# Two 64-token chunks a stage, in 64-row tiles, from stage 8 on

## The chip, the cores and the metric

The kernel runs on one core of a Trainium2 chip. The metric is the device time of one execution in microseconds. A core has five engines that run side by side: TensorE (PE, with its weight loads shown as PEld), VectorE (DVE), ScalarE (ACT), GpSimd (POOL) and SyncE (SP); DMA queues move data between the chip's memory and the core's.

## The reference

```python
# r, k, v: (batch 4, heads 8, tokens 768, 48), w, u: (8, 48), all fp32
state = np.zeros((B, H, D, D))
for t in range(S):
    cur = np.einsum('bhd,bhe->bhde', u[None] * kt, vt)
    y[:, :, t] = np.einsum('bhd,bhde->bhe', rt, state + cur)
    state = w[None, :, :, None] * state + np.einsum('bhd,bhe->bhde', kt, vt)
x = y.transpose(0, 2, 1, 3).reshape(B * S, H * D)      # 3072 tokens, 384 wide
h = x @ w_in                                           # 384 -> 2048
out = np.maximum(0.01 * h, h) @ w_out                  # 2048 -> 384
```

A linear attention with a decaying state per head (`w` the decay, `u` the weight of the token itself), then a two-layer network with a leaky rectifier over all 3072 tokens.

## The kernel before

The tokens are cut into 24 stages of 128 tokens (`L`): stage n is tokens 128 (n div 4) of batch n mod 4. So stage n + 4 takes over the state that stage n leaves. Each stage does, by its letters in the order below:

- `k`, `r`, `v` (line 241): loads, issued by GpSimd, each into a place of its own (24 places).
- `P` (390): VectorE scales r and k by powers of the decay. `X..T` (395): SyncE issues a DMA that turns both into `tp` (head dimension on the partitions); in the first stages TensorE turns them (`T`).
- `q` (419, 421, 423): VectorE forms each token's weight for itself, summed over the head dimension (`s_tok`); `Q` (430): GpSimd spreads it on the diagonal of the score tile `at`.
- `A` (482): TensorE multiplies k by r: 128x128 scores for each of 8 heads, in 8 matmuls, two of which use different halves of the rows. `M` (495): VectorE copies the part above the diagonal into `at`, two heads' halves a stage.
- `K` (523): TensorE forms the product of keys and values, 4 matmuls of 96 columns, two heads each. `S` (589, 591): VectorE adds the old state and multiplies by the decay of 128 tokens (`wl`).
- `Y` (621): TensorE forms the output, turned: 12 matmuls with the old state (`st`) as stationary operand and 16 with the values (`v_sb`), each 32 columns of the array wide and 128 columns long. `y` (635): ScalarE copies it into `xT`.
- `G`, `J` (660) and `g`, `j` (671): first layer. A `J` block is two stages (256 tokens) by two of 16 feature blocks, 6 matmuls of 256 columns; eight of them make a pair of stages. ScalarE does the rectifier.
- `H` (684) and `h` (696): second layer, one stage, 16 matmuls of 384 columns; ScalarE copies the result out, SyncE stores it.

From stage 8 on the stages go in pairs. A pair is: scores of both stages, `H`, outputs of both, key-value products of both, `H`, eight `J` blocks; from pair 7 on the scores come after the third `J`. Pairs are numbered by half their first stage: pair 4 is stages 8 and 9, pair 11 is stages 22 and 23. Stages 20 to 23 need no key-value product, since nothing follows them.

The program is written out in one list, `ORDER`; every engine runs its own instructions in the order of that list, and a small planner (`Sched`) puts in the semaphore waits: what reads waits for its writer, what writes for writer and readers. TensorE's results go to 8 banks, handed out at build time in the order of the list: `take` pops the front of a queue, `give` appends to its end. A bank is reused when its last reader is done.

```python
free = list(range(8))
def take():
    i = free.pop(0)
    return ps[i], ("ps", i)
def give(key):
    free.append(key[1])
```

Of the kernel before, what the change touches and what calls it, by code (L numbers as in the profile page):

```python
# [6 lines left out]
ALU = mybir.AluOpType  # L7
# [6 lines left out]
L = 128  # L14
# [11 lines left out]
TURNED, DIAG, CARRY, EXACT, RAW = 6, 4, 4, 1, 1  # L26
# [3 lines left out]
Q0 Y0 t3k P0k r3 P3q M1a T3q r2 P2q y0 k2 K0 M1b v1 Q1 W G0.1 Y1 t3q X3 wi3 A3 y1 g0.1 S3 T2q D3 G1.1 g1.1 k5 t2q r5 r4  # L30
P2k T2k wi2 S0 v2 M3b t2k Q3 G0.3 g0.3 G1.3 k4 M3a Y3 P5k A2 y3 P4q T4q v4 wi0 T5k v5 wo3 t4q g1.3 G3.1 q5 t5k Q5 G3.3
g3.3 P5q r6 wo2 X2 g3.1 M2b D2 wo1 G3.2 Q2 G0.2 g0.2 T5q t5q K2 P4k T4k M2a t4k S2 G1.2 g3.2 q4 Q4 K1 S1 Y2 A5 A4 G1.0
y2 G2.1 M5a G0.0 G2.3 M4a M5b Y5 g0.0 y5 M4b Y4 y4 G2.2 g2.2 K4 J2.4 j2.4 k6 wo0 J2.1 J2.2 g1.0 g1.2 S4 k7 P6q q6 j2.1
P6k P7k G2.0 r7 q7 X6T J2.6 j2.6 J2.3 j2.3 k8 G3.0 J2.7 j2.7 k9 r9 j2.2 J2.5 P7q g3.0 g2.3 X7T J2.0 H1 h1 r8 q8 g2.0 Q6
P9k j2.0 P8k H0 j2.5 H3 Q7 A6 P9q X9T P8q X8T v6 A7 M6a v7 M7a g2.1 H2 h2 v9 v11 v10 M6b Y6 M7b y6 Q8 q9 Y7 y7 K5 r11
K6 S6 r10 k10 S5 Q9 v8 K7 S7 h0 h3 k11 J3.0 j3.0 J3.1 j3.1 J3.2 j3.2 J3.3 j3.3 J3.4 j3.4 J3.5 j3.5 J3.6 j3.6 J3.7 j3.7
A8 A9 M8a M8b M9a M9b P10q P10k X10T P11q P11k X11T k12 r12 v12 k13 r13 v13 q10 Q10 q11 Q11 H4 h4 Y8 Y9 y8 y9 K8 K9 S8
S9 H5 h5 J4.0 j4.0 J4.1 j4.1 J4.2 j4.2 J4.3 j4.3 J4.4 j4.4 J4.5 j4.5 J4.6 j4.6 J4.7 j4.7 A10 A11 M10a M10b M11a M11b
P12q P12k X12T P13q P13k X13T k14 r14 v14 k15 r15 v15 q12 Q12 q13 Q13 H6 h6 Y10 Y11 y10 y11 K10 K11 S10 S11 H7 h7 J5.0
j5.0 J5.1 j5.1 J5.2 j5.2 J5.3 j5.3 J5.4 j5.4 J5.5 j5.5 J5.6 j5.6 J5.7 j5.7 A12 A13 M12a M12b M13a M13b P14q P14k X14T  # L40
P15q P15k X15T k16 r16 v16 k17 r17 v17 q14 Q14 q15 Q15 H8 h8 Y12 Y13 y12 y13 K12 K13 S12 S13 H9 h9 J6.0 j6.0 J6.1 j6.1
J6.2 j6.2 P16q P16k X16T P17q P17k X17T A14 A15 J6.3 j6.3 M14a M14b M15a M15b k18 r18 v18 k19 r19 v19 J6.4 j6.4 J6.5
j6.5 J6.6 j6.6 J6.7 j6.7 q16 Q16 q17 Q17 H10 h10 Y14 Y15 y14 y15 K14 K15 S14 S15 H11 h11 J7.0 j7.0 J7.1 j7.1 J7.2 j7.2
P18q P18k X18T P19q P19k X19T A16 A17 J7.3 j7.3 M16a M16b M17a M17b k20 r20 v20 k21 r21 v21 J7.4 j7.4 J7.5 j7.5 J7.6
j7.6 J7.7 j7.7 q18 Q18 q19 Q19 H12 h12 Y16 Y17 y16 y17 K16 K17 S16 S17 H13 h13 J8.0 j8.0 J8.1 j8.1 J8.2 j8.2 P20q P20k
X20T P21q P21k X21T A18 A19 J8.3 j8.3 M18a M18b M19a M19b k22 r22 v22 k23 r23 v23 J8.4 j8.4 J8.5 j8.5 J8.6 j8.6 J8.7
j8.7 q20 Q20 q21 Q21 H14 h14 Y18 Y19 y18 y19 K18 K19 S18 S19 H15 h15 J9.0 j9.0 J9.1 j9.1 J9.2 j9.2 P22q P22k X22T P23q
P23k X23T A20 A21 J9.3 j9.3 M20a M20b M21a M21b J9.4 j9.4 J9.5 j9.5 J9.6 j9.6 J9.7 j9.7 q22 Q22 q23 Q23 H16 h16 Y20 Y21
y20 y21 H17 h17 J10.0 j10.0 J10.1 j10.1 J10.2 j10.2 A22 A23 J10.3 j10.3 M22a M22b M23a M23b J10.4 j10.4 J10.5 j10.5
J10.6 j10.6 J10.7 j10.7 H18 h18 Y22 Y23 y22 y23 H19 h19 J11.0 j11.0 J11.1 j11.1 J11.2 j11.2 J11.3 j11.3 J11.4 j11.4  # L50
J11.5 j11.5 J11.6 j11.6 J11.7 j11.7 H20 h20 H21 h21 H22 h22
# [92 lines left out]
def bass_rwkv5_eagle__then__act_leaky_relu_kernel(  # L144
# [19 lines left out]
    r_sb = SB("r_sb", [128, NST, HD])  # L164
    k_sb = SB("k_sb", [128, NST, HD])
    v_sb = SB("v_sb", [128, NST, H * E])
# [34 lines left out]
    sum_t = [SB(f"sum_t{i}", [128, NP, 2 * D]) for i in range(4)]  # L201
    xT = [SB(f"xT{i}", [128, NSL, 512]) for i in range(NX)]
# [31 lines left out]
    def load_one(n, which, pace=()):  # L234
        b, t0 = at_of(n)
        src = {"k": k, "r": r, "v": v}[which][b].rearrange("h t d -> t h d")[t0:t0 + L, :, :]
        if which == "v":
            dst = v_sb[:, n, :].rearrange("p (h e) -> p h e", e=E)[:, :, 0:D]
        else:
            dst = {"k": k_sb, "r": r_sb}[which][:, n, :].rearrange("p (h d) -> p h d", d=D)  # L240
        add("pool", lambda: G.dma_start(dst, src), R=pace, W=[(which, n)], dma=f"{which}{n}")  # L241
# [66 lines left out]

    def zero_v(n0, n1):
        add("dve", lambda: V.memset(v_sb[:, n0:n1, :].rearrange("p n (h e) -> p (n h) e", e=E)[:, :, D:E], 0.0),  # L310
            W=[("v0", n) for n in range(n0, n1)])
# [36 lines left out]
    def table(dst, exps, name, read):  # L348
        add("act", lambda: A.activation(dst[:, :], lnw[:, :], AF.Exp, scale=exps[:, 0:1]),
            R=["lnw", read], W=[name + "tab"])  # L350
# [30 lines left out]
    def k_of(n):  # L381
        return k_sb[:, n, :] if n >= EXACT else k_f[:, n, :]

    def r_of(n):
        return r_sb[:, n, :] if n >= EXACT else r_f[:, n, :]

    def prep_half(n, half):
        iq = n % NQK
        src, tab, name, done = ((r_of(n), qtab, "r", "qp"), (k_of(n), ktab, "k", "kp"))[half]
        add("dve", lambda: V.tensor_tensor(qk[iq][:, H * half:H * half + H, 0:D], hd(src), hd(tab[:, :]), ALU.mult),  # L390
            R=[(name, n), "qk"[half] + "tab", ("qk0", iq)], W=[(done, iq)])
# [16 lines left out]
    def scaled_v(n):  # L408
        iv = n % NVS
        ps_s, key = y_bank[n]  # L410
        s_of = ps_s[:, HD:HD + H]
        add("dve", lambda: V.tensor_tensor(hd(vs[iv][:, :]),
                                           v_sb[:, n, :].rearrange("p (h e) -> p h e", e=E)[:, :, 0:D],
                                           s_of.unsqueeze(2).to_broadcast([128, H, D]), ALU.mult),
            R=[("v", n), key], W=[("vs", iv)])
# [10 lines left out]
    def diag_tile(n):  # L426
        ia = n % NAT
        for hh in range(2):
            s_of = s_tok[n % 4][:, :].rearrange("p (m two) -> p two m", two=2)[:, hh, :]
            add("pool", lambda hh=hh, s_of=s_of: G.tensor_tensor(  # L430
                at[ia][:, hh, :, :], ident[:, :].unsqueeze(1).to_broadcast([128, NP, 128]),
                s_of.unsqueeze(2).to_broadcast([128, NP, 128]), ALU.mult),
                R=["ident", ("s", n % 4)], W=[("at", ia, hh)])

# [81 lines left out]
    def kv_mm(n):  # L516
        iq = n % NQK
        ps_kv, key = kv_bank[n] = take()
        carried = NB <= n < CARRY

        def emit():
            for p in range(NP):
                last = PE.matmul(ps_kv[:, 96 * p:96 * p + 96],  # L523
                                 qk[iq][:, H + 2 * p:H + 2 * p + 2, :].rearrange("p h e -> p (h e)"),
                                 v_sb[:, n, :].rearrange("p (h e) -> p h e", e=E)[:, 2 * p:2 * p + 2, 0:D],
                                 start=p == 0 or not carried, stop=not carried)
            if carried:
                last = PE.matmul(ps_kv[:, 0:HD], ident[:, :], st[n % NT][:, :, :].rearrange("p m e -> p (m e)"),
                                 start=False, stop=True)
            return last  # L530

        reads = [("kp", iq), ("v", n), ("qk0", iq)]
        if carried:
            reads += [("st", n % NT), "ident"]
        add("pe", emit, R=reads, W=[key])
# [37 lines left out]
    def decay_table():  # L573
        for hh in range(2):
            rows = slice(64 * hh, 64 * hh + D)
            add("act", lambda rows=rows, hh=hh: A.activation(
                wl[rows, :, hh * D:hh * D + D], wcol[rows, :].unsqueeze(2).to_broadcast([D, NP, D]), AF.Exp,
                scale=float(L)), R=["wcol", "wl"], W=[f"wl{hh}"])

    def state(n):  # L580
# [4 lines left out]
        if n < NB or n < CARRY:  # L585
            add("dve", lambda: V.tensor_tensor(new[:, :, :], kv, wl[:, :, :], ALU.mult),
                R=[key, "wl0", "wl1"], W=[("st", (n + NB) % NT)])
        else:
            add("dve", lambda: V.tensor_tensor(sum_t[n % 4][:, :, :], kv, st[n % NT][:, :, :], ALU.add),  # L589
                R=[key, ("st", n % NT)], W=[("sum", n % 4)])  # L590
            add("dve", lambda: V.tensor_tensor(new[:, :, :], sum_t[n % 4][:, :, :], wl[:, :, :], ALU.mult),  # L591
                R=[("sum", n % 4), "wl0", "wl1"], W=[("st", (n + NB) % NT)])

    def y_mm(n, ps_y, key):
        it, ia, iv, is_ = n % NTP, n % NAT, n % NVS, n % NT

        def strip(s, q):
# [5 lines left out]
            if kk < 2:  # L603
                one.append((v_sb[:, n, c0 + 32 * kk:c0 + 32 * kk + 32], at[ia][:, 0, p, :]))
            if kk > 0:
                c1 = c0 + 16 + 32 * kk
                one.append((v_sb[:, n, c1:c1 + 32], at[ia][:, 1, p, :]))
# [17 lines left out]
        reads = [("v", n), ("v0", n), ("at", ia, 0), ("at", ia, 1), "ident", ("tp", it, 0)]  # L625
# [64 lines left out]
    def g2_out(n, c0=0, c1=HD):  # L690
# [20 lines left out]
        "v0y": lambda: zero_v(NB, NST), "zr": zero_raw, "qk0": zero_qk, "wlz": zero_w,  # L711
# [3 lines left out]
        "Wl": log_columns, "C": decay_columns, "W": decay_table,  # L715
# [15 lines left out]
        "L": lambda n, x: load_stage(n),  # L731
# [73 lines left out]
```

## Time and profile before

| | us |
|---|---|
| median of 3 runs | 169.3 (169.16 to 169.36) |
| span of the profiled execution, first to last instruction | 166.8 |

The page gives the span and no other time for the profiled execution; the median is 2.5 us above it.

| engine | busy us | share of the span | instructions |
|---|---|---|---|
| TensorE, matmuls | 160.2 | 96% | 2076 |
| TensorE, weight loads | 120.6 | 72% | 2076 |
| VectorE | 107.6 | 64% | 224 |
| ScalarE | 89.0 | 53% | 168 |
| GpSimd | 111.0 | 67% | 125 |

How to read the lines that follow: a group line gives line and engine, operation, output and inputs, the shapes and the count, then busy us and the mean ns of one, then the engine's idle time in front of them and what ended it. The lines of the chain and of the timeline begin with the start in us and the length in us; several equal instructions in a row are one line (x16). Matmuls are pipelined: the length of one (some 0.2 us) is not what it costs, the distance between starts is. The granted clock of TensorE is full in all forty slices of the page but for rounding.

### The profile page before, as it was taken

What the parts mean: (1) busy time and instruction counts of PE and PEld (TensorE: products, weight loads), DVE (VectorE), ACT (ScalarE), POOL (GpSimd) and SP (SyncE); (2) the same over time, 40 slices, a digit from 0 to 9 for tenths busy, and PEclk for the clock granted to TensorE, in tenths of its full rate; (3) what the DMA queues carried; (4) which work ended last, traced back from release to release, by engine and by line L of the source; (5) the groups of instructions that cost most, each with busy time, mean ns of one, the idle gap of its engine ahead of it and who ended that gap; (6) DMA issues with size and microseconds to landing.
All of it is one profiled execution on the core that took longest, in us unless ns stands there. A gap on an engine that the chain in (4) does not pass through costs nothing.

```text
span 166.8 us, 4840 instructions
## 1 busy us (share of the span) xinstructions
PE 160.2 (96%) x2076; PEld 120.6 (72%) x2076; DVE 107.6 (64%) x224; ACT 89.0 (53%) x168; POOL 111.0 (67%) x125
## 2 busy tenths in 40 slices
PE   2899989999999999999999999999999999999994
PEld 2578879986567678678678678678678678678663
DVE  7799998478687695695699998865765705000000
ACT  3846973875048339339337437437437447449121
POOL 8999898978999949859759979896630630000000
PEclk9999999999999999999999999999999999999999
DMA  7999999999999994996994999999917011011012
GB/s 109 156 140 157 169 193 192 171 149 173 93 168 220 113 157 130 105 108 155 105 146 118 152 127 127 156 140 140 154 51 165 12 47 51 0 47 51 35 59 96
DMA packets 101267, 20.18 MB, mean 121 GB/s; under 512 B 94459, under 2 KB 101246, under 8 KB 101246
## 3 DMA queue, kind: packets, MB, share of 16 engines
q0 software_dynamic: 76512, 10.03, 95.0%
q1 hardware_dynamic: 23694, 9.65, 29.1%
q8 instruction: 16, 0.26, 0.7%
q10 hardware_dynamic: 1040, 0.20, 0.6%
q14 instruction: 5, 0.04, 0.1%
HBM read 20.45 MB, written 4.72 MB: 151 GB/s over the span
## 4 chain that ended last, share of the span: by engine, by line
PE 86%; POOL 7%; DMA 3%; DVE 2%; issue 0%; ACT 0%; POOLq 0%
PE ps L684 38%; PE ps L660 36%; PE ps L621 6%; DMA r_sb<-in_r_dram 3%; PE ps L482 3%; PE ps L523 2%; POOL r_sb L241 2%; POOL k_sb L241 2%; POOL v_sb L241 2%; POOL w_in_sb L251 1%; DVE prod L405 1%; DVE s_tok L423 0%; PE ps L453 0%; POOL trow L273 0%; DVE rku L421 0%
## 5 line engine op out<-in xcount | busy, mean ns | idle before, releaser
L660 PE MATMUL ps<-xT,w_in_sb 128*128 128x256 bf16 (+1 forms) x672 | 67.2, 257 | 0.0
L684 PE MATMUL ps<-w_out_sb,gT 128*128 128x384 bf16 (+2 forms) x400 | 65.6, 320 | 0.0
L671 ACT ACTIVATE gT<-ps 128x512 bf16<-128x512 f32 x96 | 56.3, 598 | 13.8 <-PE ps L660 9.7
L660 PEld LDWEIGHTS ps<-xT,w_in_sb 128*128 128x128 bf16 x672 | 57.1, 98 | 7.5 <-DVE sum_t L589 0.5
L430 POOL TENSOR_TENSOR at<-ident,s_tok 128x512 bf16<-128x512 bf16 x40 | 42.7, 1096 | 23.4 <-DVE s_tok L423 23.4
L684 PEld LDWEIGHTS ps<-w_out_sb,gT 128*128 128x128 bf16 x400 | 37.7, 98 | 22.4
L696 ACT ACTIVATE out_sb<-ps 128x384 f32<-128x384 f32 (+2 forms) x25 | 11.8, 477 | 54.5 <-PE ps L684 54.5
L495 DVE CAST_PREDICATED at<-mask,ps 128x512 bf16<-128x512 uint16 x40 | 24.9, 684 | 21.3 <-PE ps L482 21.2
L241 POOL DMA_DIRECT2D v_sb<-in_v_dram x24 | 22.1, 927 | 0.0
L241 POOL DMA_DIRECT2D k_sb<-in_k_dram x23 | 21.2, 925 | 0.0
L241 POOL DMA_DIRECT2D r_sb<-in_r_dram x23 | 21.1, 924 | 0.1
L421 DVE TENSOR_TENSOR rku<-r_sb,ku 128x384 bf16<-128x384 bf16 x20 | 13.8, 688 | 1.1 <-DMA r_sb<-in_r_dram 0.5
L589 DVE TENSOR_TENSOR sum_t<-ps,st 128x384 bf16<-128x384 f32 x16 | 8.8, 550 | 5.6 <-PE ps L523 5.6
L635 ACT ACTIVATE xT<-ps 128x384 bf16<-128x384 f32 x24 | 10.8, 490 | 2.6 <-PE ps L621 2.6
L423 DVE TENSOR_REDUCE s_tok<-rku 128x8 f32<-128x384 bf16 x20 | 11.1, 553 | 0.7
L591 DVE TENSOR_TENSOR st<-sum_t,wl 128x384 bf16<-128x384 bf16 x16 | 10.6, 664 | 0.6
L621 PE MATMUL ps<-at,v_sb 128*32 128x128 bf16 x384 | 10.8, 223 | 0.0
L390 DVE TENSOR_TENSOR qk<-k_sb,ktab 128x384 bf16<-128x384 bf16 x23 | 10.1, 444 | 1.1 <-DMA k_sb<-in_k_dram 1.1
L621 PEld LDWEIGHTS ps<-tp,st 128*32 128x32 bf16 x240 | 7.3, 96 | 3.0 <-issue 1.6
L621 PEld LDWEIGHTS ps<-at,v_sb 128*32 128x32 bf16 x384 | 8.8, 98 | 0.5 <-issue 0.2
L621 PE MATMUL ps<-tp,st 128*32 128x128 bf16 x240 | 9.1, 221 | 0.0
L390 DVE TENSOR_TENSOR qk<-r_sb,qtab 128x384 bf16<-128x384 bf16 x23 | 8.8, 386 | 0.2 <-DMA r_sb<-in_r_dram 0.2
(63 smaller groups left out, 92.9 us busy)
## 6 DMA issues: line engine op xcount, KB each, us to landing
out_dram<-out_sb SPq DMA_DIRECT2D x23, 192.0 KB, 2.2
v_sb<-in_v_dram POOLq DMA_DIRECT2D x24, 96.0 KB, 4.8
r_sb<-in_r_dram POOLq DMA_DIRECT2D x23, 96.0 KB, 4.7
k_sb<-in_k_dram POOLq DMA_DIRECT2D x23, 96.0 KB, 4.9
w_in_sb<-in_moe_w_in_dram POOLq DMA_DIRECT2D x4, 384.0 KB, 6.1
w_out_sb<-in_moe_w_out_dram POOLq DMA_DIRECT2D x4, 384.0 KB, 7.1
tp<-qk SPq DMA_TRANSPOSE x18, 5.3
k_f<-in_k_dram ACTq DMA_DIRECT2D x1, 192.0 KB, 2.8
```

The source lines that it names most:

```text
L241: add("pool", lambda: G.dma_start(dst, src), R=pace, W=[(which, n)], dma=f"{which}{n}")
L390: add("dve", lambda: V.tensor_tensor(qk[iq][:, H * half:H * half + H, 0:D], hd(src), hd(tab[:, :]), ALU.mult), R=[(name, n), "qk"[half] + ...
L421: add("dve", lambda: V.tensor_tensor(rku[i2][:, :], r_of(n), ku[i2][:, :], ALU.mult), R=[("r", n), ("ku", i2)], W=[("rku", i2)])
L423: add("dve", lambda: V.tensor_reduce(s_tok[i2][:, :], hd(rku[i2][:, :]), AX.X, ALU.add), R=[("rku", i2)], W=[("s", i2)])
L430: add("pool", lambda hh=hh, s_of=s_of: G.tensor_tensor(at[ia][:, hh, :, :], ident[:, :].unsqueeze(1).to_broadcast([128, NP, 128]), s_of.un ...
L495: add("dve", lambda: V.copy_predicated(at[n % NAT][:, hh, :, :], mask[:, :].bitcast(mybir.dt.uint16).unsqueeze(1).to_broadcast([128, NP, 1 ...
L621: last = PE.matmul(ps_y[32 * q:32 * q + 32, 128 * s:128 * s + 128], a, m, start=not whole and step == 0, stop=step == len(columns[q]) - 1)
L635: add("act", lambda: A.activation(xT[ix][:, :, 128 * slot:128 * slot + 128], ps_y[:, 0:HD].rearrange("p (s t) -> p s t", t=128), AF.Copy), ...
L660: last = PE.matmul(ps_g[:, step * f:step * f + step], w_in_sb[:, s, 128 * fb:128 * fb + 128], xT[ix][:, s, t], start=s == 0, stop=s == NSL ...
L671: add("act", lambda: A.activation(gT[ig][:, fb0:fb0 + count, t], ps_g[:, :].rearrange("p (f t) -> p f t", t=128 * width), AF.Prelu, alpha= ...
L684: last = PE.matmul(ps_o[:, 0:c1 - c0], gT[ig][:, s, 128 * slot:128 * slot + 128], w_out_sb[:, s, c0:c1], start=s == 0, stop=s == NFB - 1)
L696: add("act", lambda: A.activation(out_sb[io][:, c0:c1], ps_o[:, 0:c1 - c0], AF.Copy), R=[key], W=held)
```

## The change

From stage 8 on a stage is worked as two chunks of 64 tokens, with a state between them; two stages are handled together.

- Scores (`AA`): only the two 64x64 blocks on the diagonal are formed, 32 matmuls of 64x64 tiles by 64 columns a pair in place of 16 of 128 by 128. One mask operation (`MM`) covers both stages, so two a pair in place of four; the diagonal tiles on GpSimd have half the elements.
- Key-value products (`KK`): one for each chunk, 32 matmuls of 64x64 tiles by 48 columns a pair in place of 8 of 96; only the products of a head with itself. For stages 20 to 23 that of the first chunk is formed, where there was none. They come right after the scores, ahead of the outputs.
- State (`SM` after the first chunk, `SO` after the second): sum, product with the decay of 64 tokens in fp32, half as wide, and two copies that spread it to the old form for the outputs. Four a pair in place of two, of four operations (five for the first of stages 8 to 11) in place of two.
- Outputs (`YY`): 48 matmuls a pair with the states as stationary operand (128 rows, 32 columns wide, 64 long) in place of 24 of 128, then 64 with the values (64 rows, 32 wide, 64 long) in place of 32 of 128. The two chunks go to different banks.
- Order: the scores come after the fourth `J` block in all pairs; the preparation `P` and the transposes for the next pairs stand ahead of the scores from pair 5 on.
- Loads of k, r and v go into rings of 16 places, so stage n waits for the readers of stage n - 16.
- Before stage 8: tables of powers for 64-token chunks (`qtab2`, `ktab2`, `wlc`, `wl2`), a smaller mask and identity, and six memsets.

TensorE's matmuls go from 2076 to 2828. The order of one period before (pair 6) and after (pair 5):

```diff
-A12 A13 M12a M12b M13a M13b P14q P14k X14T P15q P15k X15T k16 r16 v16 k17 r17 v17 q14 Q14 q15 Q15 H8 h8
-Y12 Y13 y12 y13 K12 K13 S12 S13 H9 h9 J6.0 j6.0 J6.1 j6.1 ...
+J4.0 j4.0 J4.1 j4.1 J4.2 j4.2 P12q P12k X12T P13q P13k X13T J4.3 j4.3 AA5 KK5 J4.4 j4.4 MM5a MM5b SM10 SM11
+k14 r14 v14 k15 r15 v15 J4.5 j4.5 J4.6 j4.6 J4.7 j4.7 q12 Q12 q13 Q13 SO10 SO11 H6 h6 YY5 yy5a yy5b H7 h7
```

```diff
-            dst = v_sb[:, n, :].rearrange("p (h e) -> p h e", e=E)[:, :, 0:D]
+            dst = v_sb[:, n % NR, :].rearrange("p (h e) -> p h e", e=E)[:, :, 0:D]
...
-        add("pool", lambda: G.dma_start(dst, src), R=pace, W=[(which, n)], dma=f"{which}{n}")
+        add("pool", lambda: G.dma_start(dst, src), R=pace, W=[(which, n), (which, n - NR)], dma=f"{which}{n}")
...
+    def a_pair(j):
+        at_bank["pair", j] = (take(), take())
+        def emit():
+            for i in range(2):
+                it = (2 * j + i) % NTP
+                for p in range(NP):
+                    for hh in range(2):
+                        rows = slice(64 * hh, 64 * hh + D)
+                        for c in range(2):
+                            t = slice(64 * c, 64 * c + 64)
+                            x = 64 * (NP * i + p)
+                            last = PE.matmul(at_bank["pair", j][hh][0][t, x:x + 64], tp[it][rows, NP + p, t],
+                                             tp[it][rows, p, t], start=True, stop=True)
+            return last
...
+    def kv_pair(j):
+        chunks = range(2 if 2 * j + NB < NST else 1)
+        kv_bank["pair", j] = [take() for _ in chunks]
...
+                        for hh in range(2):
+                            t, x = slice(64 * c, 64 * c + 64), D * (NP * i + p)
+                            h = 2 * p + hh
+                            last = PE.matmul(kv_bank["pair", j][c][0][64 * hh:64 * hh + 64, x:x + D],
+                                             qk[n % NQK][t, H + h, :], v_sb[t, n % NR, E * h:E * h + D],
+                                             start=True, stop=True)
...
+    def half_state(n, c):
...
+            add("dve", lambda: V.tensor_tensor(both[:, :, :], kv, old[:, :, :], ALU.add), ...
...
+        add("dve", lambda: V.tensor_tensor(new[:, :, :], both[:, :, :], wlc[:, :, :], ALU.mult), ...
+        blocks(wide, new, name, at_)          # two copies of 64 partitions
+        if i == 1:
+            give(key)
...
+    def y_pair(j):
+        y_bank["pair", j] = (take(), take())
...
+                        for q in range(4):
+                            p, kk = divmod(4 * s + q, 3)
+                            mm(c, i, s, q, old[:, p, 32 * kk:32 * kk + 32], tp[n % NTP][:, p, 64 * c:64 * c + 64], False)
...
+                for step in range(4):
+                    for c in range(2):
+                        t = slice(64 * c, 64 * c + 64)
+                        for q in range(4):
+                            s, hh, c0, p = lists[q][step]
+                            last = mm(c, i, s, q, v_sb[t, n % NR, c0:c0 + 32], tile[t, hh, NP * i + p, :],
+                                      i == 1 and step == 3)
```

More of the change, by code (lines that the diff above doesn't have):

```diff
@@ L163, in bass_rwkv5_eagle__then__act_leaky_relu_kernel @@
     w_out_sb = SB("w_out_sb", [128, NFB, HD])
[L164 to L166 removed]
+    r_sb = SB("r_sb", [128, NR, HD])
+    k_sb = SB("k_sb", [128, NR, HD])
+    v_sb = SB("v_sb", [128, NR, H * E])
     w_row = SB("w_row", [128, HD // 2], FP32)
@@ new lines, in a_pair @@
+    def a_pair(j):
[12 more added lines that the diff above has]
+            return last
+        add("pe", emit, R=[("tp", (2 * j + i) % NTP, half) for i in range(2) for half in range(2)],
+            W=[key for _, key in at_bank["pair", j]])
```

234 lines of the change are left out of this document (179 added, 55 removed).

## The prediction

> **What bounds the kernel now.** I read the page first, then the chain of waits in order of time, then busy time by window, then the timeline of TensorE down to single groups of matmuls.
>
> ```profile
> span 166.8 us, 4840 instructions
> ...
> PE 160.2 (96%) x2076; PEld 120.6 (72%) x2076; DVE 107.6 (64%) x224; ACT 89.0 (53%) x168; POOL 111.0 (67%) x125
> ```
>
> The page says that TensorE is busy 96% of the span. A busy share can hide waits, so I look at one period of the part that the change touches. The chain in order of time, start and length in us:
>
> ```profile
> 95.78 0.89 PE ps L621 x56
> 96.67 0.45 PE ps L523 x8
> 97.12 2.60 PE ps L684 x16
> 99.72 1.97 PE ps L660 x18
> 101.68 0.55 PE ps L482 x16
> 102.24 3.38 PE ps L660 x30
> ...
> 108.22 0.90 PE ps L621 x56
> ```
>
> From one L621 (attention output) to the next it is all TensorE: 12.44 us for two stages, no other engine in the chain. Each piece fits a price per column. L684 streams 384 columns in 2.60/16 = 162.5 ns, L660 256 columns in 1.97/18 = 109.4 ns: 0.415 ns a column and some 3 ns fixed. So a 64-column matmul would stream in 29.6 ns. The four-up groups come from the timeline (start, length, count):
>
> ```profile
> 83.56 0.22 PE L621 MATMUL ps<-tp,st 128*32 128x128 bf16 x1
> 83.61 0.23 PE L621 MATMUL ps<-at,v_sb 128*32 128x128 bf16 x4
> 83.67 0.23 PE L621 MATMUL ps<-tp,st 128*32 128x128 bf16 x4
> ...
> 84.16 0.51 PE L523 MATMUL ps<-v_sb,qk 128*128 128x96 bf16 x8
> 84.51 2.76 PE L684 MATMUL ps<-w_out_sb,gT 128*128 128x384 bf16 x16
> ```
>
> Four matmuls into four 32-column strips last 0.23 us together where one lasts 0.22: they run side by side, one group each 56 ns (83.61 to 83.67). The 56 matmuls of L621 are 14 groups, 0.78 us; their piece is 0.89, so some 0.10 us is lost where the shape of the tiles changes. The 16 of L482 are 8 pairs at 56 ns, 0.45 us, and the piece is 0.55: the same 0.10. L523 takes (84.51 - 84.16)/8 = 43 ns each, 0.345 us. The check: L660 48 x 109.4 = 5.25, L684 32 x 162.5 = 5.20, scores 0.45, outputs 0.78, key-value 0.345, four changes of shape 0.40, sum 12.43 against 12.44. The stretch has no idle time to win back; only matmul time counts, and a wait that is added counts in full.
>
> **The change part by part.** The terms of the sum are made against the span of 166.8 us; the page gives this execution no time of its own beside it. The median of the runs is 169.3, so 2.5 us lie outside the span and I keep them.
>
> *Matmuls.* In groups that run at once, for a pair of stages. Scores: from 8 groups of two tiles by 128 columns to 8 groups of four 64x64 tiles by 64 columns. Key-value: from 8 single matmuls by 96 to 8 groups of four 64x64 tiles by 48. Outputs, state part: from 6 groups of four by 128 to 12 groups of four by 64. Outputs, value part: from 8 groups of four by 128 to 8 groups of eight 64x32 tiles by 64. Changes of shape: from four to five, the new one inside the outputs (128 rows to 64). All of it lies on the path. What a group of the new shapes costs the trace doesn't show. Below it is bounded by a matmul that streams 2 columns, above by the 56 ns of the groups that exist.
>
> ```profile
> 15.59 0.24 PE L510 MATMUL ps<-wu,prod 128*128 128x2 bf16 x4
> 15.70 0.23 PE L660 MATMUL ps<-xT,w_in_sb 128*128 128x128 bf16 x1
> ```
>
> ```profile
> 83.26 0.10 PEld L621 LDWEIGHTS ps<-tp,st 128*32 128x32 bf16 x4 [0.32 <-issue]
> 83.27 0.24 PE L621 MATMUL ps<-tp,st 128*32 128x128 bf16 x4
> 83.28 0.10 PEld L621 LDWEIGHTS ps<-at,v_sb 128*32 128x32 bf16 x4
> ```
>
> The first fence is from an early stretch: four 2-column matmuls, each with its own stationary load, take 15.70 - 15.59 = 0.11 us, 27 ns each: nothing in the trace shows a load and a matmul of one tile follow faster. So 27 to 56 ns. The second is the start of an L621 burst, loads and matmuls. [...]
>
> For the 32-wide tiles I take 30 ns: their loads follow one another within 20 ns (the two rows of loads at 83.26 and 83.28), so the 29.6 ns of streaming should decide. For the 64-wide tiles I take 40 ns: the load is twice as wide, has to follow the previous matmul of its tile, and was so far hidden behind 43 to 56 ns; nearer to the 27 ns row than to the 56 ns one, since a 128-wide load already fits in it.
>
> Pairs 4 to 9: scores 8 x (56 - 40) = 0.13 us less; key-value 0.345 - 8 x 0.040 = 0.025 less; outputs 14 x 56 - 20 x 30 = 0.18 less; one more change of shape, 0.10 more. Net -0.24, times six -1.4 us. Pairs 10 and 11 had no key-value product (their state was never needed) and now need the one between the chunks: 0.32 more, so -0.13 + 0.32 - 0.18 + 0.10 = +0.11 each, +0.2. Sum of TensorE -1.2 us. With 29.6 ns everywhere it is 6 x -0.41 + 2 x -0.06 = -2.6 us.
>
> *VectorE.* Two masks a pair instead of four, but the state step runs four times a pair (twice a stage), each a sum, a product and two half-height copies.
>
> ```profile
> L495 DVE CAST_PREDICATED at<-mask,ps 128x512 bf16<-128x512 uint16 x40 | 24.9, 684 | 21.3 <-PE ps L482 21.2
> ...
> L589 DVE TENSOR_TENSOR sum_t<-ps,st 128x384 bf16<-128x384 f32 x16 | 8.8, 550 | 5.6 <-PE ps L523 5.6
> ...
> L591 DVE TENSOR_TENSOR st<-sum_t,wl 128x384 bf16<-128x384 bf16 x16 | 10.6, 664 | 0.6
> ```
>
> ```profile
> 52.45 0.55 DVE L589 TENSOR_TENSOR sum_t<-ps,st 128x384 bf16<-128x384 f32 x1
> 53.03 0.36 DVE L591 TENSOR_TENSOR st<-sum_t,wl 128x384 bf16<-128x384 bf16 x1
> ...
> 58.04 0.35 DVE L390 TENSOR_TENSOR qk<-r_sb,qtab 128x384 bf16<-128x384 bf16 x1
> ...
> 59.11 0.35 DVE L419 TENSOR_TENSOR ku<-k_sb,u_tab 128x384 bf16<-128x384 bf16 x1
> ...
> 62.33 0.55 DVE L589 TENSOR_TENSOR sum_t<-ps,st 128x384 bf16<-128x384 f32 x1
> ```
>
> ```profile
> sum 49.77, PE 49.77 PEld 36.98 DVE 39.98 ACT 26.44 POOL 41.27; mean PE 12.44 PEld 9.25 DVE 10.00 ACT 6.61 POOL 10.32
> ```
>
> The three views: groups by line (count, busy, mean ns), timeline, and busy time by window, whose last row is the mean over four such periods: VectorE is busy 10.0 of 12.44 us. From 550 ns for 384 and 684 for 512 columns a column costs 1.05 ns, so a 192-column sum takes 350 ns. The product takes at most the 360 ns of the row at 53.03, a copy between half of that and all of it, I take 250; an operation that waits for the one before it starts 30 ns after its end (0.58 against 0.55). A step is 1.24 us, with ends at 0.8 (halves throughout) and 1.66 (580 and three times 360). So 10.0 - 2 x 0.684 - 2 x (0.55 + 0.664) + 4 x 1.24 = 11.2 us, against a period of 12.2. It fits, nothing is paid, with 1 us to spare.
>
> Two waits go with it. The outputs wait for the middle state, which has four J blocks and one H block before it (5.2 us); behind the outputs stands everything on TensorE. And the second chunk's key-value bank stays taken until the sum of the second state, which VectorE does after the row sums; by the order of the banks the last L660 block before the next scores (J 3) takes it again. That sum ends 1.37 (masks) + 2 x 1.24 + 3.2 (row sums, 59.11 to 62.33) + 1.24 + 0.38 = 8.7 us after the scores and is needed 11 us after them. The first pair has less room.
>
> *The first pair (stages 8, 9).* Its scores come after four of eight J blocks instead of after all eight, 24 x 0.109 = 2.6 us earlier.
>
> ```profile
> 67.64 0.55 PE ps L482 x16
> ```
>
> ```profile
> 58.68 2.60 SPq L395 DMA_TRANSPOSE tp<-qk  x2
> ```
>
> ```profile
> DMA to landing us min/median/max: 4.5/4.8/5.0
> ```
>
> The fences: chain in order of time, SyncE's queue, and the transposes of stages 10 and 11. SyncE's row is its two transposes. VectorE ends its old state work at 53.4 (the 53.03 row), then has six new memsets (1.2, an estimate: 192 packed columns each at the 1.05 ns above), masks (1.4), two middle states with one more add each (3.0), and only then, at 59.0, the preparation of stages 10 and 11 (58.04 to 59.11 now, 1.1): their transposes start at 59.5 and 60.8, 0.8 later than now, and land at 64.5 and 65.3. The scores of pair 5 stand at 67.64 now; four blocks and the saving of pair 4 earlier is 64.8. The bank is free at 60.1 + 3.2 + 1.24 + 0.38 = 64.9, less with shorter GpSimd tiles, and wanted one block ahead, at 64.1. So 0.5 or 0.8 us, and less where VectorE waits for GpSimd less: I put the stall at 0.4 us, between 0 and 1.2.
>
> *What costs nothing.* The diagonal tiles on GpSimd halve (40 of 1.1 us now); GpSimd is not in the chain here and waits for VectorE's row sums. The five new tables, the masks and wider memsets before stage 8 take 2 to 3 us of ScalarE and VectorE, both with idle time there. The rings of 16 make loads from stage 16 wait for readers of stage n - 16, which are done some 30 us earlier. SyncE's order of stores and transposes stays. ScalarE has the same evacuations, 6.6 of 12.4 us.
>
> Sum: -1.2 + 0.4 = -0.8 us, span 166.0, time **168.5 us**.
>
> **The rivals.**
>
> *The 64-wide load sets the pace (170.5 us, 0.12).* If a 64-wide load can't be hidden behind 29.6 ns and the 64x64 groups stay at 56 ns, scores win nothing, key-value loses 0.10 a pair and pairs 10 and 11 pay 0.45 for it: 6 x 0.02 + 2 x 0.36 = +0.8, with the stall 170.5. For it speaks that no row shows a 64-wide bf16 load; against it that the 128-wide one fits in 27 ns. [...]
>
> *TensorE issues no faster than it is seen to (the other side: slower; 178 us, 0.13).* The best sustained pace in the trace is four loads and four matmuls each 56 ns, 14 ns a matmul. There are 752 more matmuls. If 14 ns is a limit of issue and not of streaming, or eight tiles don't run at once, outputs go from 56 to 112 matmuls a pair, +0.78, key-value +0.10, the change of shape +0.10: six times +0.98, twice +1.33, +8.5 us, 178 with the stall. If only the groups stay at 56 ns, it is 174.7 (20 groups instead of 14 in the outputs, +0.34). Against it: in the rows from 83.26 to 83.28 eight loads and four matmuls start within some 30 ns. It decides from about 10 ns a matmul.
>
> *VectorE becomes the bound (170.9 to 172.3 us, 0.12).* It decides from a state step of 1.5 us (6.2 + 4 x 1.5 = 12.2). At 1.6 it costs 0.4 a pair, at the upper end of 1.66 0.64, six times: +2.4 to +3.8. The wait would stand in front of J 3, for the bank. For it: four short operations that wait for one another; against it: less contention with GpSimd, whose tiles halve.
>
> **How the numbers follow.** The forecast's mechanism (groups of 27 to 48 ns, stall under 1.2) has 0.60, the rivals 0.12, 0.13 and 0.12, 0.03 is for what I don't see. 0.2% of 169.3 is 0.34 us, about what a measurement of this kernel can tell from no change. Of the forecast's 0.60, 0.48 lies below 168.96 and 0.12 within 0.34 us of no change (40 ns and a full stall), so faster 0.48, same 0.12, slower 0.40. Low end: all groups at 29.6 ns and no stall give 166.7, a little under it is 166.5. High end 173.0: it takes in the load rival and VectorE's and leaves out the issue rival; with the little below 166.5 that is under 0.2. The likeliest case alone runs from 166.5 to 169.4.
>
> **What would show it.** In the profile after: the scores and the key-value product one piece of about 0.75 us, the outputs about 0.8, and 2828 matmuls in all. Right: a period of some 12.2 us and VectorE at 11. The load rival: 64x64 groups start 56 ns apart. The issue rival: outputs over 1.5 us. VectorE's: idle time of TensorE before L660 (in the new file the same helper), released by the sum of the state. A stall of over 1.2 us at the scores of stages 10 and 11, released by a transpose, would make the first-pair term wrong.

## The result and the profile after

The changed kernel takes 176.0 us (median of 4 runs, 175.1 to 176.9) beside 169.3 us of the kernel before (169.2 to 169.4 in the same session): 1.041 times, 95% interval 1.0365 to 1.0456. Forecast were 168.5 us and a range of 166.5 to 173.0. The sign was wrong and the range did not hold it. Times below are medians of a kernel's executions within 1.5% of its fastest, and the ratios go by the same ones.

The page of the changed kernel (the busy row has engine, busy us, share of the span, instructions; then the granted clock of TensorE in 40 slices; then the queue that brings TensorE its instructions, to judge by the counts below):

```profile
span 173.7 us, 6424 instructions
...
PE 162.9 (94%) x2828; PEld 123.3 (71%) x2828; DVE 122.6 (71%) x314; ACT 91.5 (53%) x173; POOL 98.0 (56%) x125
...
PEclk9999999999998589999999999999999999999999
...
q8 instruction: 22, 0.36, 1.0%
```

The span grew by 6.9 us, TensorE's busy time by 2.7. The clock row dips in one place, slices 13 to 15, some 52 to 65 us. The chain of waits there, in order of time, and the first periods behind it (start, length):

```profile
50.34 6.73 DMA v_sb<-in_v_dram
57.08 0.14 issue
57.21 0.63 PE ps L527 x25
57.84 4.79 PE ps L840 x24
62.63 2.60 PE ps L864 x16
65.23 1.10 PE ps L575 x112
...
71.66 0.37 PE ps L499 x32
72.03 0.26 PE ps L527 x32
72.29 2.73 PE ps L840 x24
75.02 2.60 PE ps L864 x16
77.62 1.10 PE ps L575 x112
78.71 2.71 PE ps L864 x16
81.42 2.62 PE ps L840 x24
84.04 0.37 PE ps L499 x32
```

In the kernel before, the chain is TensorE alone at this place; here it runs through a load: `v8`, issued at 50.34 behind a diagonal tile of GpSimd, lands at 57.08. L527 is the key-value product `KK4`, which the change moved from behind the outputs to right behind the scores. The kernel before issued the same load (first line, GpSimd's timeline) and read it first at the outputs, then at the product (its chain):

```profile
51.36 0.94 POOL L241 DMA_DIRECT2D v_sb<-in_v_dram  x1
...
58.46 0.90 PE ps L621 x56
59.35 0.45 PE ps L523 x8
```

There it was issued 1.0 us later, but landed after 3.7 us, at 55.1. In the changed kernel it takes 6.7 us, about the median of the 24 loads of v there (6.6; before 4.8). Why the loads are slower isn't shown. With 3.7 us the wait would have been some 0.6 us (an estimate: 50.34 + 3.7 + 0.14 against the end of the scores at 53.60).

In the changed kernel, the waits (engine, line, what it waited for: us in total, times, longest) and the timeline of the scores and the product:

```profile
PE ps L527 <- DMA v_sb<-in_v_dram: 3.6, 1, 3.6
```

```profile
53.15 0.45 PE L499 MATMUL ps<-tp 48*64 48x64 bf16 x32 [0.65 <-DMA tp<-qk]
...
57.21 0.63 PE L527 MATMUL ps<-v_sb,qk 64*64 64x48 bf16 x32 [3.62 <-DMA v_sb<-in_v_dram]
```

Busy time by window for the same place (window and its length, busy us of PE, PEld, DVE, ACT, POOL with counts, then the granted clock):

```profile
49.00:53.00 4.00, 3.49 (x44) 2.81 (x36) 3.43 (x11) 3.67 (x8) 3.79 (x5) 1.00 2.14 160
53.00:57.00 4.00, 0.45 (x32) 0.36 (x32) 1.86 (x5) 0.12 (x1) 4.00 (x6) 0.78 2.06 211
57.00:60.00 3.00, 2.79 (x43) 2.15 (x44) 1.93 (x7) 0.60 (x1) 0.41 (x1) 0.50 2.67 139
60.00:63.00 3.00, 3.00 (x19) 2.15 (x18) 2.85 (x10) 1.52 (x3) 0.00 (x0) 0.66 1.00 53
```

In finer windows the clock is still 1.00 from 53.60 to 55.00, 0.61 from 55 to 56, then 0.50 until 62 and 0.98 in the microsecond behind that: it falls during the wait, and the 24 matmuls of L840 take 4.79 us where the same 24 take 2.73 a pair later.

The rest of the kernel hardly moved. Scores and key-value products went from 0.55 + 0.45 to 0.37 + 0.26 us, the outputs from 0.89 to 1.10, the two `H` blocks from 2.60 + 2.60 to 2.60 + 2.71, the eight `J` blocks stayed at 5.35: 12.39 us a period instead of 12.44. The mean over three periods (span of the windows, then PE, PEld, DVE, ACT, POOL):

```profile
sum 37.15, PE 37.15 PEld 27.82 DVE 33.01 ACT 19.90 POOL 24.53; mean PE 12.38 PEld 9.27 DVE 11.00 ACT 6.63 POOL 8.18
```

Pairs 10 and 11, which had no key-value product before, got longer. The outputs in the chain, first of the kernel before, then of the changed one:

```profile
133.10 0.90 PE ps L621 x56
145.20 0.90 PE ps L621 x56
```

```profile
139.51 1.10 PE ps L575 x112
151.88 1.10 PE ps L575 x112
```

12.10 us before, 12.37 after. The sum: 3.6 (load) + 0.65 (scores of pair 4 for a transpose) + 2.06 (L840 at a low clock) + 0.37 (L527, 0.63 instead of 0.26) - 6 x 0.06 (pairs 4 to 9) + 2 x 0.27 is 6.9 us, the difference of the spans.

### The profile page after: what moved, and what is told of

It is laid out like the page before. It is cut to its first block, busy times and chain, and to the rows that moved or that the text cites. A ratio compares the mean times of both kernels' runs of the same rounds, so it can differ in the third digit from the quotient of the medians.

```text
span 173.7 us, 6424 instructions
## 1 busy us (share of the span) xinstructions
PE 162.9 (94%) x2828; PEld 123.3 (71%) x2828; DVE 122.6 (71%) x314; ACT 91.5 (53%) x173; POOL 98.0 (56%) x125
## 4 chain that ended last, share of the span: by engine, by line
PE 84%; DMA 6%; DVE 6%; ACT 1%; issue 1%; SPq 1%; POOL 1%; DVEq 0%
PE ps L864 35%; PE ps L840 34%; PE ps L575 5%; DMA v_sb<-in_v_dram 4%; DMA w_row<-in_w_dram 2%; PE ps L639 2%; PE ps L499 2%; PE ps L527 1%; DVE at L681 1%; PE ps L668 1%; PE ps L801 1%; DVE prod L442 1%; DVE at L677 1%; PE ps L300 1%; POOL at L482 1%
## 5 line engine op out<-in xcount | busy, mean ns | idle before, releaser
L840 PE MATMUL ps<-xT,w_in_sb 128*128 128x256 bf16 (+1 forms) x672 | 69.9, 262 | 0.1
L840 PEld LDWEIGHTS ps<-xT,w_in_sb 128*128 128x128 bf16 x672 | 58.3, 100 | 8.0 <-issue 0.3
L482 POOL TENSOR_TENSOR at<-ident,s_tok 128x256 bf16<-128x256 bf16 x32 | 20.8, 672 | 40.5 <-DVE s_tok L460 40.5
L509 DVE CAST_PREDICATED at<-mask,ps 128x512 bf16<-128x512 uint16 x16 | 10.3, 687 | 12.2 <-PE ps L499 12.0
L458 DVE TENSOR_TENSOR rku<-r_sb,ku 128x384 bf16<-128x384 bf16 x20 | 10.0, 498 | 0.7
L469 POOL TENSOR_TENSOR at<-ident,s_tok 128x512 bf16<-128x512 bf16 x8 | 8.7, 1106 | 2.9 <-DVE s_tok L460 2.9
L538 DVE CAST st<-c_in 64x192 bf16<-64x192 f32 x24 | 9.9, 413 | 0.6
L617 ACT ACTIVATE xT<-ps 128x384 bf16<-128x384 f32 x16 | 7.0, 488 | 4.7 <-PE ps L575 4.7
L456 DVE TENSOR_TENSOR ku<-k_sb,u_tab 128x384 bf16<-128x384 bf16 x20 | 8.7, 434 | 0.2
L538 DVE CAST st_mid<-c_mid 64x192 bf16<-64x192 f32 x32 | 8.1, 255 | 0.8
L527 PE MATMUL ps<-v_sb,qk 64*64 64x48 bf16 x224 | 3.6, 192 | 3.6 <-DMA v_sb<-in_v_dram 3.6
L681 DVE CAST_PREDICATED at<-mask,ps 128x512 bf16<-128x512 uint16 x8 | 5.0, 685 | 2.3 <-PE ps L668 2.2
```

The costliest lines, as they stand in the source:

```text
L456: add("dve", lambda: V.tensor_tensor(ku[i2][:, :], k_of(n), u_tab[:, :], ALU.mult), R=[("k", n), "u_tab"], W=[("ku", i2)])
L458: add("dve", lambda: V.tensor_tensor(rku[i2][:, :], r_of(n), ku[i2][:, :], ALU.mult), R=[("r", n), ("ku", i2)], W=[("rku", i2)])
L482: add("pool", lambda hh=hh, s_of=s_of: G.tensor_tensor(tile[:, hh, NP * i:NP * i + NP, :], ident2[:, :].unsqueeze(1).to_broadcast([128, NP ...
L509: add("dve", lambda: V.copy_predicated(tile[:, hh, :, :], mask2[:, :].bitcast(mybir.dt.uint16).unsqueeze(1).to_broadcast([128, 2 * NP, 64] ...
L538: add("dve", lambda rows=rows, hh=hh: V.tensor_copy(dst[rows, :, D * hh:D * hh + D], src[rows, :, :]), R=[read], W=[write])
L840: last = PE.matmul(ps_g[:, step * f:step * f + step], w_in_sb[:, s, 128 * fb:128 * fb + 128], xT[ix][:, s, t], start=s == 0, stop=s == NSL ...
```

## The experiments

Theory: the order of pair 4 costs it, a wait for `v8` and the clock after it, and the tiles are about even. Rival: the small tiles cost it all along.

**The load alone.**

```diff
-H2 h2 v9 v11 v10 ... Q9 v8 K7
+H2 h2 v8 v9 v11 v10 ... Q9 K7
```

> The changed kernel with one load moved: v of stage 8 is issued by GpSimd ahead of those of stages 9, 11 and 10 instead of behind the diagonal tile of stage 9. Theory (the loss is the key-value product of pair 4, which waits 3.6 us for that load, and the 24 matmuls after it at a lower clock, 2.1 us): no wait of L527 for a load, granted clock back near 1.0, 169 to 169.8 us. Rival (the small tiles cost it all along the kernel): still above 174 us.

170.4 us, 1.0104 times the kernel before (1.0067 to 1.0142). The wait and the dip of the clock are gone, and with them three quarters of the loss; the rival falls. Some 1.7 us are left, more than the 0.5 I had allowed. This is the window of 57 to 60 us, with the clock at 1.00, and what stands in its waits of TensorE:

```profile
57.00:60.00 3.00, 2.77 (x63) 1.62 (x60) 2.81 (x9) 0.85 (x2) 0.43 (x1) 1.00 2.70 141
```

```profile
PE ps L575 <- DVE st_mid L538: 0.5, 2, 0.3
...
PE ps L840 <- DVE sum_c L554: 0.3, 1, 0.3
```

The outputs of pairs 4 and 5 wait for the middle state, and a `J` block of pair 4 for a bank that the second state holds (its matmuls start 0.46 us late there).

**The order alone, old tiles.** The kernel before, with pair 4 reordered:

```diff
-J3.3 j3.3 J3.4 j3.4 ... J3.7 j3.7 A8 A9 M8a ... Y8 Y9 y8 y9 K8 K9 S8 S9
+J3.3 j3.3 A8 A9 K8 K9 J3.4 j3.4 M8a ... Y8 Y9 y8 y9 S8 S9
```

> The kernel before with its old tiles, and in pair 4 alone the new order: scores of stages 8 and 9 after four of eight blocks, their key-value products right behind. Theory (order, not tiles): TensorE waits for v of stage 8 there. That load is issued at 51.4 and the products could start at about 52.8, so a wait of 2.3 us if it lands in 3.7 us as it does in this kernel, 4.5 us if in 6.7 as in the changed one, and up to 2 us of lower clock behind it: 171.5 to 176 us. Rival (tiles): 169.3 us, within 0.4.

173.0 us, 1.0251 (1.0205 to 1.0298): slower by 4.2 us with not one tile changed. Its timeline:

```profile
54.07 0.62 PE L482 MATMUL ps<-tp 48*128 48x128 bf16 x16 [0.78 <-DVE sum_t L589]
...
56.25 0.50 PE L523 MATMUL ps<-v_sb,qk 128*128 128x96 bf16 x8 [1.56 <-DMA v_sb<-in_v_dram]
```

The same wait for the same load, here 1.6 us in an execution of 172.1 us, the fastest of four (to 174.2), beside 0.8 us in which the scores wait for a bank. Behind it the clock stays at 1.00:

```profile
57.00:59.00 2.00, 1.97 (x19) 1.52 (x18) 1.93 (x8) 1.23 (x3) 2.00 (x3) 1.00 2.13 117
```

The other three executions, which have no trace, were granted 0.99 in the mean, so in them the clock may have fallen for a short time, and the 4.2 us can hold some of that.

**The clock apart from the wait.** Two kernels keep TensorE busy for the first 3.2 us of its wait, with matmuls whose results nobody reads.

```diff
-AA4 KK4
+AA4 F54 KK4        # 54 of 128 columns; in the second kernel 14 of 512
```

> The changed kernel as it is, with 54 matmuls of 128 columns on a constant tile (about 3 us) between the scores and the key-value products of pair 4, where TensorE waits 3.6 us for the load; their results are not used. Theory (part of the loss is the clock that drops after the idle time): the 24 matmuls behind the wait take 2.7 instead of 4.8 us, granted clock 1.0, 1.5 to 2.2 us less than the changed kernel, 173.8 to 174.5 us. Rival (those matmuls were slow for another reason, such as traffic on memory): no difference, 176 us.

> The changed kernel with TensorE kept busy during its wait in pair 4, this time by 14 matmuls of 512 columns (some 3 us; results not used) instead of 54 of 128, so that the instructions behind move by 28 places instead of 108. Theory (clock): the 24 matmuls behind the wait take 2.7 instead of 4.8 us at a granted clock of 1.0 and, with no stop of TensorE at later outputs for instructions, the time falls by 1.5 to 2.2 us: 173.8 to 174.5 us at 169.3 of the kernel before, ratio 1.027 to 1.031. Rival (the clock is no part of the loss, or is paid again later): ratio 1.040 or more, as for the changed kernel and the kernel with 54 fillers.

The first: 176.3 us, 1.0436 (1.0382 to 1.0489), no gain. The second: 173.3 us, 1.0248 (1.022 to 1.0276), 2.7 us less than the changed kernel, a little more than expected (the traced execution is the slowest of its four, with a span 1.1 us shorter). Both traces show the clock at 1.00 behind the wait; this is the chain of the second, then its wait for the load and the window of 57 to 60 us:

```profile
50.22 7.94 DMA v_sb<-in_v_dram
...
58.29 0.44 PE ps L537 x32
58.73 2.73 PE ps L850 x24
```

```profile
PE ps L537 <- DMA v_sb<-in_v_dram: 2.2, 1, 2.2
```

```profile
57.00:60.00 3.00, 1.71 (x45) 1.57 (x46) 1.11 (x4) 0.47 (x1) 0.29 (x1) 1.00 2.68 141
```

2.73 us for the 24 matmuls, as in any later pair, though here the load landed 1.1 us later and TensorE still sat idle for 2.2 us before the product. The traffic was the same in that window (last number, 141 GB/s beside 139 in the changed kernel). The clock is so shown as a part of the loss, and the rival falls. The product itself takes 0.44 us here at a full clock, not 0.26, so of its 0.37 us in the sum above only 0.19 are the clock. That the first kernel gained nothing had other reasons: its load landed 0.8 us later than in the changed kernel, and this stands in its chain at the outputs of pair 8:

```profile
113.45 1.09 PE ps L575 x111
114.53 1.51 issue
116.04 0.19 PE ps L575
```

111 of 112 matmuls, then 1.5 us in which TensorE waits for nothing that the profile shows, then the last one.

**What limits the outputs.** They take 1.10 us for 112 matmuls where I forecast 0.8. In two kernels with the load moved, the value part goes first; in the second the `H` block stands between the parts.

```diff
-for i: for s: for c: for q: mm(state ...)      # 48 matmuls of 128x32 tiles
-for i: for step: for c: for q: mm(value ...)   # 64 matmuls of 64x32 tiles
+value loop, then state loop                    # first kernel
+YV4 H4 h4 YS4 instead of H4 h4 YY4             # second kernel
```

> The load moved as in the first run, and the outputs' value part (64-row tiles) ahead of their state part (128-row tiles). Theory that instructions come to TensorE at 8.3 ns a matmul once a queued store is used up: the value part, now at the head of the burst, starts its groups of eight 29 to 40 ns apart for four groups or more, the state part's groups take 33 ns, the piece stays 1.05 to 1.15 us, time within 0.4 us of the first run. Rival that the 64-row tiles themselves run no faster than 8.3 ns a matmul: the value part still takes 0.53 us or more from its start and the state part's groups stay at 29 ns.

> The load moved as in the first run, and the outputs cut in two: value part ahead of the 16 matmuls of 384 columns, state part behind them, in the same banks. Theory of the instruction supply: the store of queued instructions fills up during those 2.6 us, so value part 0.30 to 0.42 us and state part 0.36 to 0.42, together 0.7 to 0.85 instead of 1.10 with changes of shape included, period 12.15 to 12.25 instead of 12.38, 1 to 2 us less than the first run. Rival (tiles limit): value part 0.55 or more, another change of shape of 0.1, so 0.5 to 1 us more than the first run.

The first: 170.2 us, 1.0086 (1.0057 to 1.0115), as the kernel with the load moved. Its value part in two windows of the outputs' line (length, PE, PEld with their counts, clock):

```profile
96.48:96.61 0.13, 0.12 (x32) 0.13 (x32) 1.00 1.57 142
96.71:96.97 0.26, 0.26 (x55) 0.25 (x31) 1.00 1.75 152
```

32 loads with their matmuls start in 0.13 us, four groups of eight some 30 ns apart; then comes a break of 0.1 us; then 31 pairs need 0.26 us, 8.3 ns each. So a 64x32 tile can run at 30 ns a group of eight, and the first 32 pairs do; those behind the break come at 8.3 ns each. In the changed kernel the state part, which goes first there, shows the same with other tiles: its groups start 29 ns apart, so 33 loads last longer and there is no break, but its 34th load comes 0.24 us after its first, as the value part's does (0.23), and from there on the loads are 8.3 ns apart in both. So neither the pace nor the break belongs to the 64x32 tiles or to the passage from the pair's first stage to its second, which falls at the same matmul. The rival (the tiles themselves) falls. The theory's pace of 8.3 ns is measured; its store of instructions would fit, but no row shows one, and the state part's groups at 33 ns did not come: ten of its twelve start 29 ns apart.

The split kernel did not gain: 173.0 us, 1.0207 (1.0155 to 1.0259). Its parts take 0.61 and 0.48 us, together 1.09 and not 0.85 at most. The value part's length is the rival's number, but it is what the windows above add up to: 32 pairs in 0.13 us, the break of 0.1, 32 pairs at 8.3 ns (0.27) and a change of shape of 0.1. Cut in two, the parts are 0.01 us shorter together than in one piece, and both `H` blocks take 2.71 us, where in the changed kernel the first takes 2.60. Beside that a new loss stands in its timeline, in pair 4:

```profile
56.53 0.63 PE L571 MATMUL ps<-at,v_sb 64*32 64x64 bf16 x57
58.58 0.11 PEld L571 LDWEIGHTS ps<-at,v_sb 64*32 64x32 bf16 x7 [1.54 <-issue]
58.58 0.22 PE L571 MATMUL ps<-at,v_sb 64*32 64x64 bf16 x7 [1.43 <-issue]
```

**Instructions in blocks.** The queue q8 of the page above moved 22 packets of 0.36 MB, 16 KB each; before, it was 16 packets for 2076 matmuls. The 752 matmuls more have as many loads, 1504 instructions for six packets, and 1504 / 6 is 251 a packet. The split kernel, also of 2828 matmuls, moved 22 packets too. The stops of the split kernel's value parts (pairs 4 to 7) and those of the first filled kernel (pairs 8 and 9) all fall at the same count of TensorE's instructions but for whole blocks of 256, to within two. So 256 instructions to a packet is the estimate here, from these counts and the 251. The next kernel moves the split kernel's stream against the blocks and changes nothing else behind the start:

```diff
-F9 ... F6 ... F4                # 19 matmuls of 128 columns
+F47 ... F31 ... F21             # 99 matmuls of 2 columns
```

> The kernel with the outputs cut in two around the 16 matmuls of 384 columns, which stopped for 1.4 and 0.4 us in the value parts of pairs 4 and 6 with nothing to wait for but instructions. Only change: the 19 warming matmuls of 128 columns at the start of the kernel are 99 of 2 columns, some as long together, so all later instructions of TensorE stand 160 places further back. Theory (TensorE fetches its instructions in blocks of 16 KB, 256 instructions, and stops where a block ends inside the short dense run of scores, key-value products and values before the next one is there): the stops in pairs 4 and 6 are gone and the breaks over 0.1 us in the value parts of pairs 5 and 7 too, 1.5 to 2.5 us less, ratio 1.006 to 1.012. Rival (the stops belong to these matmuls, their banks or tiles): stops at the same matmuls, ratio 1.02.

170.9 us, 1.0137 (1.0105 to 1.017), 1.2 us less by the ratios and 2.1 us by the spans (171.1 and 169.0). The intervals of the two kernels overlap, so it is the trace that decides. The stops are gone from the value parts; this is pair 5 in its chain:

```profile
69.33 0.61 PE ps L572 x64
```

The stops move with the count of TensorE's instructions, as the theory of the blocks has it; the rival (banks or tiles) falls. That TensorE waits there for the next block is my reading: the profile names no cause. The ratio is a little above the range that I gave: the split form keeps a change of shape more, 12.49 us a period. A stop of 0.4 us remains in a `J` block right behind the products of pair 4; it too falls at the same count.

**Fewer instructions in the outputs.** The value part in 128-row tiles, 80 matmuls a pair. `SO8 SO9` ahead of the row sums and the zeroings of the middle states ahead of `M6a` came first, as a kernel of their own:

```diff
-A7 M6a ... q10 Q10 q11 Q11 SO8 SO9
+A7 smz M6a ... SO8 SO9 q10 Q10 q11 Q11          # both kernels
+mm(i, q, 128 * s, 128, v_sb[:, n % NR, c0:c0 + 32], at[n % NAT][:, hh, p, :], ...)  # second kernel
```

> The first run's kernel, and VectorE's queue around the first pair relieved: the four zeroings of the middle states (0.84 us) stand ahead of the masks of stage 6, where VectorE waits 3.4 us for TensorE, and the second states of stages 8 and 9 stand ahead of the row sums of stages 10 and 11. Theory: the 1.1 us by which the first run stays behind the kernel before are the waits of the first two pairs for VectorE (0.3 us at the outputs and 0.46 at a bank in pair 4, 0.3 at the outputs of pair 5), the rest of the change being even: 1.002 to 1.006 of the kernel before. Rival: that loss lies in the matmuls of all pairs: stays at 1.010.

> The kernel of the run above, with the value part of the outputs in 128-row tiles (32 matmuls of 128 columns on a block-diagonal score tile instead of 64 of 64 columns), so 80 instead of 112 matmuls and no change of shape inside the outputs. GpSimd makes its diagonal tiles in full width again, VectorE masks in eight pieces a pair of 64 rows by 256 columns, ScalarE does the copies of the states. Theory (outputs are bound by the supply of instructions, 8.3 ns a matmul, and the change of shape): outputs 0.85 to 0.95 us instead of 1.10, VectorE 10 to 10.6 and ScalarE about 9 of a period of 12.15 to 12.25 us, 1.2 to 1.6 us less than the run above, so 0.994 to 0.999 of the kernel before. Rival: the longer masks or the copies on ScalarE come late and set the pace: period 12.4 or more, no gain.

The first: 169.8 us, 1.0058 (1.0034 to 1.0082), by the midpoints half of what was left, though its interval overlaps that of the first run. TensorE's waits of pair 4 are gone, that of pair 5 has grown to 0.6 us:

```profile
PE ps L577 <- DVE st_mid L540: 0.6, 1, 0.6
```

The second: 176.6 us, 1.0443 (1.0398 to 1.0488), far off, and by the rival. Its VectorE masks (groups by line) and the outputs in its timeline:

```profile
L514 DVE CAST_PREDICATED at<-mask,ps 64x256 bf16<-64x256 uint16 x64 | 26.9, 420 | 12.3 <-PE ps L501 7.9 <-PE ps L533 2.6
```

```profile
102.02 0.21 PE L581 MATMUL ps<-tp,st 128*32 128x64 bf16 x4 [0.53 <-ACT st_mid L544]
```

A mask of 64 rows by 256 columns takes 420 ns, so the eight of a pair take 3.4 us where two of 128 by 512 took 1.4 (687 ns each in the changed kernel). They stand ahead of the middle state, in the chain followed by its sum and product (0.8 us) and ScalarE's copies (1.5 us); the outputs wait for these in every pair (7.0 us over the eight), and a period takes 12.8 us. Their piece did fall, from 1.10 to 1.01 us, half of the fall that I expected.

**All that helped.** The kernel with the load and VectorE mended, the value part ahead of the state part with a wait for each; in the first of two kernels also the preparation of stages 12 and 13 behind the middle states.

```diff
-YY4 ...
+YV4 YS4 ...                                   # both, in all pairs
-P12q P12k X12T P13q P13k X13T ... SM10 SM11
+... SM10 SM11 P12q P12k X12T P13q P13k X13T   # first only
```

> The kernel with v of stage 8 early and VectorE relieved, and two edits more: the outputs' value part ahead of the state part with a wait of its own for each, so that only the state part waits for the middle state; and in pair 5 the preparation of stages 12 and 13 behind the middle states of stages 10 and 11. Theory (what is left over the kernel before is the wait of 0.65 us for the middle state at the outputs of pair 5, and the tiles as such are even): 0.5 to 0.8 us less, 0.999 to 1.003 of the kernel before. Rival (the small tiles or their number of instructions cost more than the trace of one run shows): 1.005 or more.

> The kernel of the run with all edits but one: the preparation of stages 12 and 13 stands where the change put it, ahead of the masks of pair 5. Kept are v of stage 8 early, VectorE relieved in pair 4, and the value part ahead of the state part with a wait for each. Theory (the moved preparation only made the transposes of stages 12 and 13 late, 0.4 us, and the value part now covers 0.5 of the 0.65 us for which pair 5 waited for the middle state): 0.998 to 1.003 of the kernel before, even with it. Rival (the tiles cost more than shown): 1.005 or more. A gain over the kernel before needs the period of 12.38 us to weigh more than the two last pairs, which cost 0.27 us each; I expect none.

The first: 169.6 us, 1.0034 (1.0008 to 1.0060); the second: 169.5 us, 1.0012 (0.9984 to 1.0041), no difference from the kernel before that shows. So with the waits mended the small tiles are even with the old ones to within 0.4%, as the theory has it. Of its details one fell: in the trace of the second, TensorE still waits for the middle state,

```profile
PE ps L574 <- DVE st_mid L541: 0.5, 1, 0.5
```

so the value part covered little of that wait, and why this kernel is 0.4% nearer than the one with VectorE alone relieved (their intervals overlap) stays open. No version beat the kernel before.

## Why the prediction was wrong, point by point

- **The first pair.** Here it failed. This part named the transposes of stages 10 and 11 and a bank, and put 0.4 us on them. It did not ask what the moved key-value product waits for: `v8` stood at the end of GpSimd's list, behind `Q9`, and had been early enough only because in the kernel before its first readers, the outputs, start at 58.46. Of the loss, 3.6 us are that wait, made longer by a load that took 6.7 us instead of 3.7, and some 2.2 the clock behind it. Nor did the part look at the transposes of stages 8 and 9, for which the scores of pair 4 wait 0.65 us. The waits that the part did name were 1.1 us with the load out of the way (0.3 and 0.46 in pair 4, 0.3 in pair 5), within its 0 to 1.2, and their causes were the named ones and the outputs' wait for the middle state.
- **What costs nothing** spoke of the rings' loads from stage 16 only. Those cost nothing. The load of stage 8 was not looked at.
- **Matmuls, 64-wide tiles.** 40 ns a group was forecast. Scores and products start 32 matmuls in 0.26 us, 32 ns a group (for the products, the rows of the chain from 72.03 to 72.29; in their second half single loads come 8 ns apart, so there the pace of the outputs' later matmuls, 8.3 ns, can set it). The load rival (56 ns) is out. Scores and products gained 0.37 us a pair where 0.155 was forecast.
- **Matmuls, outputs.** This term was mis-sized: 1.10 us instead of 0.8. 30 ns a group holds for most of the state part and for the first 25 to 32 matmuls of a value part; the rest come at 8.3 ns each, 66 ns for eight where the forecast's estimate for eight side by side was 29.6, with a break of 0.1 us in between. The issue rival came nearest, a pace per matmul, measured at 8.3 ns and not its 14, and it decides at 8.3, not "from about 10 ns": what scores and products win (0.37 us) the outputs (0.21) and the change of shape ahead of the second `H` (0.11) give back for the most part. A period gained 0.06 us instead of 0.24.
- **Pairs 10 and 11** lost 0.27 us each, forecast 0.11. So all matmul terms came to some +0.2 us (-6 x 0.06 + 2 x 0.27) instead of -1.2; the last kernel is even with the kernel before.
- **VectorE.** 11.2 us a period forecast, 10.9 to 11.3 measured, and it is not the bound; that rival is out, though in pairs 4 and 5 TensorE waits for it.

## What to carry to other kernels

When a step is moved up in a written-out order, list everything it waits for, loads first, and look when each was issued and landed: a load that was early enough for the old place has no price in the old profile, and its time to landing can differ in the new one (3.7 and 6.7 us here). Look at the granted clock behind an added wait too: after 3.6 us of idle time it was 0.50 here, and the 24 matmuls that came next took 2.1 us longer. When matmuls are cut into more and smaller ones, count instructions: in the outputs here TensorE came down to 8.3 ns a matmul past a burst of some 32, and dense runs stopped, for up to 1.5 us, at the same count of instructions but for blocks of 256.

## What was not expected of the hardware

- In the outputs the first 32 loads with their matmuls start 4 ns apart (0.13 us for 32), those behind the break 8.3 ns apart. A store of instructions that is used up is my reading; no run shows it by itself.
- The packets of q8 are of 16 KB, by the counts some 251 loads and matmuls each, and TensorE stopped for up to 1.5 us at the same count of its instructions but for blocks of 256, inside dense small matmuls or right behind them. With the stream moved by 160 instructions against the blocks, the stops were gone from the value parts. What TensorE waits for at such a stop isn't shown.
- 3.6 us of idle time, with 0.65 us shortly before, brought the granted clock to 0.50 in the changed kernel and cost 2.1 us over the next 24 matmuls (4.79 us instead of 2.73); 1.6 us in one trace and 2.2 to 2.3 us in those of the two filled kernels left it at 1.00. What decides between them no run here separates.
